# A load of two input tiles moved into the middle of five transposed weight loads, and a fourth matmul pair moved behind a tile's last one

## The chip, the cores and the metric

The kernel runs on one core of one Trainium2 chip. Its time is the device time of one execution in microseconds: 271.55 us, the median of three runs (271.33 to 272.35). The profile shows another view of one execution: which engine did what, counted from the span's first instruction.

The engines are TensorE (PE for its matmuls, PEld for its weight loads), VectorE (DVE), ScalarE (ACT), GpSimd (POOL) and SyncE (SP). SP computes nothing here; it issues nearly all DMAs, one after the other, and the core's 16 DMA engines carry them out. Every DMA of this kernel's SP queue is split into 16 pieces, one for each DMA engine, and has landed when the last piece has.

## The reference, cut to what matters

One transformer block over x (2048 rows of 640, bf16): linear attention with 32 heads of 20 columns, then a gated feed-forward network.

```python
qkv = layernorm(x) @ wqkv                  # q, k, v: 32 heads x 20 columns
pq, pk = q @ w_phi, k @ w_phi              # per head, 20 x 20
phi_q = concat(softmax(pq), softmax(-pq));  phi_k = concat(softmax(pk), softmax(-pk))
kv = phi_k.T @ v;  z = sum of phi_k over the rows
o = (phi_q @ kv) / (phi_q @ z + 1e-6)
h = x + o @ wo
h2 = h + (gelu(layernorm(h) @ w_gate) * (layernorm(h) @ w_up)) @ w_down
```

## The kernel before, in words

The 2048 rows are 16 tiles of 128 rows, kept in SBUF as four groups `x_sb[0..3]` of four tiles; tiles 6 and 7 are `x_sb[1][:, 2:4, :]`. The work has three stages: k and v of all tiles (about the first 58 us), then the queries, the attention and the feed-forward network, in which attention of later tiles is woven between the feed-forward matmuls.

The change lies in the opening of the first stage. Since `w_phi` follows W_k directly, the kernel multiplies the two once, on the chip: `fold` (L232) takes the transposed W_k (`WkT`, loaded by `load_T`, L200 to L205) and writes the product to `Wk2`. WkT comes in five blocks of 128 rows, each by one transposing DMA of SP (L203). `fold(WkT, Wk2, False, (d,))` needs block d alone: six matmuls into a PSUM tile `wa` (L248), whose loaded weights are the block, and then one copy into chunk d of `Wk2`, by ACT for chunks 0, 1, 3 and 4 (L257) and by DVE for chunk 2 (L259). k of a tile is a sum over the five chunks of `Wk2`: `k_part(t, c)` (L326) issues the two matmuls of chunk c (L296, two halves of 320 columns) of tile t, so it can begin while later chunks are not folded yet. `k_tile(t)` (L331) issues chunk 4, which ends k of the tile, and ACT takes the two exponentials of the result (L340).

TensorE and SP run in the order in which the program is written (`manual_schedule`, L81), and so do the others inside L82. TensorE's order around the change is: fold 0, 1, 2; v of tile 3 (ten matmuls); fold 3; chunks 0 to 2 of k of tile 0 and chunk 0 of tile 1 (eight matmuls); fold 4; chunks 1 and 2 of k of tile 1, chunk 3 of tile 0, chunk 3 of tile 1, chunk 4 of tile 0, chunk 4 of tile 1; then v of tile 4, k of tile 2 and so on in turn.

SP's order is: x tiles 0 to 2, W_v in three loads, x tile 3 among them, x tiles 4 and 5, the five blocks of WkT, x tiles 6 and 7 (L470), the transposed load of the normalized tile 4 (L167, called from `ln_ap`), x tiles 8 and 9 (L475), the normalized tile 5, x tiles 10 and 11 (L487), the normalized tile 6, and so on. The transposed loads of L167 each wait for the normalization of their tile (by DVE or ACT); the loads of x wait for nothing but SP. Tiles 6 and 7 are first read by the statistics of `ln_st(6)` and `ln_st(7)` on DVE (L488, L489; the instructions have L121).

Of the kernel before, what the change touches and what calls it, by code (L numbers as in the profile page):

```python
# [17 lines left out]
def kernel(  # L18
# [12 lines left out]
    nc = tc.nc  # L31
# [8 lines left out]
    NC = D // P  # L40
# [32 lines left out]
    x_v = A_x.rearrange("b (p t) d -> p (b t) d", t=NT)  # L73
# [11 lines left out]
    x_sb = [const.tile([P, 4, D], BF16, name=f"x_sb{b}") for b in range(NB)]  # L85
# [25 lines left out]
    def gtile(name):  # L111
        return psG.tile([P, 2, 512], F32, name=name, tag="G")
# [46 lines left out]
    def transpose_to(dst, src, on_pe, on_dve=False):  # L159

        if on_pe:
            tp = psG.tile([P, 16, P], BF16, name="tp", tag="G")
            for c in range(NC):
                nc.tensor.transpose(tp[:, c, :], src[:, c * P:(c + 1) * P], ident)  # L164
            (nc.vector.tensor_copy if on_dve else nc.scalar.copy)(dst, tp[:, 0:NC, :])  # L165
        else:
            nc.sync.dma_start_transpose(dst, src)  # L167
# [15 lines left out]
    WkT = fp.tile([P, NC, D], BF16, name="WkT")  # L183
# [16 lines left out]
    def load_T(WT, i, *ds):  # L200

        for d in ds:
            nc.sync.dma_start_transpose(WT[:, :, d * P:(d + 1) * P], A_wqkv[d * P:(d + 1) * P, i * D:(i + 1) * D])  # L203

    load_T(WkT, 1, *range(NC))  # L205
    wo_v = A_wo.rearrange("(c p) n -> p c n", p=P)
    wg_v = B_w_gate.rearrange("(c p) n -> p c n", p=P)
    wu_v = B_w_up.rearrange("(c p) n -> p c n", p=P)
# [23 lines left out]
    def fold(WT, W2, quarters, ds=range(NC)):  # L232


        n, w = 1, HD
        runs = []
        for c in range(NC):
            lo, hi = H0[c] * Dh, (H0[c] + NH[c]) * Dh
            for r in range(2 * n):
                a, b = max(lo, r * w), min(hi, (r + 1) * w)  # L240
                if a < b:
                    runs.append((r // n, r, c, a, b))
        runs.sort()
        for d in ds:
            wa = gtile("wa")
            wr = wa.rearrange("p u (q x) -> p (u q) x", q=n)
            for i, (u, r, c, a, b) in enumerate(runs):
                nc.tensor.matmul(wr[:, r, a - r * w:b - r * w], lhsT=WT[:, c, d * P:(d + 1) * P],  # L248
                                 rhs=BD[:, c].rearrange("p a b -> p (a b)")[:, a - H0[c] * Dh:b - H0[c] * Dh],
                                 start=(i == 0 or runs[i - 1][0] != u),  # L250
                                 stop=(i + 1 == len(runs) or runs[i + 1][0] != u), skip_group_check=True)
            dst, src = W2[:, d, :].rearrange("p (u f) -> p u f", u=2), wr[:, :, 0:w]
            if quarters:
                dst = W2[:, d, :].rearrange("p (c u m f) -> p u m c f", c=NC, u=2, m=2)
                src = src.rearrange("p u (m c f) -> p u m c f", m=2, c=NC)
            if d in (QA if quarters else KA):
                nc.scalar.copy(dst, src)  # L257
            else:
                nc.vector.tensor_copy(dst, src)  # L259
# [15 lines left out]
    def ln_st(*tiles, act=True, between=None, log=False):  # L275
        for t, v in zip(tiles, ln_stats(p1, [x_sb[t // 4][:, t % 4, :] for t in tiles], "1", act, between, log)):
            lnp[t] = v

    def ln_ap(t, on_act=False, on_pe=False):
        ln = (ln_act if on_act else ln_dve)(p1, "1", *lnp[t])  # L280
        if on_pe:
            lnp[t] = ln
        else:
            transpose_to(LN1T[t // 4][:, :, t % 4 * P:(t % 4 + 1) * P], ln, False)

    def ln_tp(t, on_dve=False):
        transpose_to(LN1T[t // 4][:, :, t % 4 * P:(t % 4 + 1) * P], lnp[t], True, on_dve)
# [5 lines left out]
    def proj(ps, t, W, us=(0, 1), cs=None):  # L293
        order = [(u, c) for u in us for c in range(NC)] if cs is None else [(u, c) for c in cs for u in us]
        for u, c in order:
            nc.tensor.matmul(ps[:, u, 0:HD], lhsT=lnT(t, c), rhs=W[:, c, u * HD:(u + 1) * HD],  # L296
                             start=(c == 0), stop=(c == NC - 1))
# [3 lines left out]
    def v_mm(t, us=(0, 1)):  # L301
        if 0 in us:
            pv[t] = gtile("pv")
        proj(pv[t], t, Wv, us)
# [10 lines left out]
    def v_ev(t):  # L315
        nc.scalar.activation(vS[t % NV][:, :, 1:VC].rearrange("p (u h) f -> p u h f", u=2),
                             pv[t][:, :, 0:HD].rearrange("p u (h f) -> p u h f", f=Dh), ACTF.Copy,
                             scale=lnp[t][2] if t in CT else 1.0)
# [7 lines left out]
    def k_part(t, *cs):  # L326
        if 0 in cs:
            pks[t] = gtile("pk")
        proj(pks[t], t, Wk2, cs=cs)

    def k_tile(t):  # L331
        if t in pks:
            pk = pks[t]
            k_part(t, NC - 1)
        else:
            pk = gtile("pk")
            proj(pk, t, Wk2)
        Ek[t] = ev.tile([P, 2, D], BF16, name="E", bufs=10)
        for s in range(2):
            nc.scalar.activation(Ek[t][:, s, :].rearrange("p (u f) -> p u f", u=2), pk[:, :, 0:HD],  # L340
                                 ACTF.Exp, scale=((lnp[t][2], nrstd[t]) if t in CT else (1.0, -1.0))[s])
# [26 lines left out]
    def kv_tile(t):  # L368

        E = Ek[t].rearrange("p s (h f) -> p s h f", f=Dh)  # L370
        for i in range(QH):
            for r in range(4):
                h = r * QH + i
                nc.tensor.matmul(kvp[QUAD[r], :, i * Dh:(i + 1) * Dh], lhsT=vF[t % NV][:, h * VC:h * VC + 32],  # L374
                                 rhs=E[:, :, h, :], start=(i == t == 0), stop=(t == NT - 1), skip_group_check=True)
# [11 lines left out]
    def q_mm(j, part=(0, 1), kcs=range(NC)):  # L387

        if 0 in part and 0 in kcs:
            pqs[j] = gtile("pq")  # L390
        for i, bc in enumerate(QG[j]):
            if i not in part:
                continue
            b, c = divmod(bc, NC)
            for kc in kcs:
                nc.tensor.matmul(pqs[j][:, i, :], lhsT=Wq2[:, kc, c * P:(c + 1) * P], rhs=LN1T[b][:, kc, :],  # L396
                                 start=(kc == 0), stop=(kc == NC - 1))

    def q_exp(j, signs=(0, 1)):
        for s in signs:  # L400
            nc.scalar.activation(Eq[j][:, :, s, :], pqs[j][:, 0:len(QG[j])], ACTF.Exp, scale=(1.0, -1.0)[s])  # L401
# [13 lines left out]
    def ln_a(t):  # L415

        ln = p1.tile([P, D], BF16, name="ln1", bufs=3)
        nc.vector.tensor_scalar(ln, x_sb[0][:, t, :], va[t][:, 0:1], va[t][:, 3:4], op0=ALU.add, op1=ALU.mult)
        return ln
# [47 lines left out]
                                op0=ALU.mult, op1=ALU.add)  # L467
    ln_st(4, act=False, between=lambda: ln_ap(3, on_pe=True))
    ln_tp(3, True)
    nc.sync.dma_start(x_sb[1][:, 2:4, :], x_v[:, 6:8, :])  # L470
    v_ev(2)
    fold(WkT, Wk2, False, (0,))
    fold(WkT, Wk2, False, (1,))
# [8 lines left out]
    fold(WkT, Wk2, False, (4,))  # L482
    k_part(1, 1, 2)
    k_part(0, 3)
    k_part(1, 3)
    ln_ap(5)
    nc.sync.dma_start(x_sb[2][:, 2:4, :], x_v[:, 10:12, :])  # L487
    ln_st(6)  # L488
# [5 lines left out]
    for t in range(NT):  # L494
        if t == T3:
            kvp = gtile("kvp")[:, 0, 0:2 * QF].rearrange("p (s f) -> p s f", s=2)
        late = t in (1, 2, 3, 4)
        if 0 < t < NT - 6 and not late:
            ln_ap(t + 6, on_act=True)
        k_tile(t)  # L500
        if t == 0:
            ln_ap(6)
            nc.sync.dma_start(x_sb[3][:, 0:2, :], x_v[:, 12:14, :])
        if t in FQ:
            fold(WqT, Wq2, True, [i for i, f in enumerate(FQ) if f == t])
        for i in KVG.get(t, ()):
            kv_tile(i)
        for j in range(len(QT)):
            if t == QT[j]:
                q_mm(j)  # L510
                q_exp(j)
                if j == 0:
                    nc.gpsimd.tensor_copy(Wg[:, 0, 0:1], Eq[j][:, 0, 1, 0:1])
                for i in KVQ.get(j, ()):
                    kv_tile(i)
        if 0 < t < NT - 3:
            v_mm(t + 3)
        if late:
            ln_ap(t + 6, on_act=True)
        if t == 1:  # L520
            nc.sync.dma_start(x_sb[3][:, 2:4, :], x_v[:, 14:16, :])
        if 0 < t < NT - 3:
            v_ev(t + 3)
        for i in ST.get(t, ()):
            ln_st(i, i + 1)
        k_norm(t)
        load_T(WqT, 0, *[i for i, f in enumerate(LQ) if f == t])
        if t == 10:
            transpose_to(LN1T[0][:, :, P:2 * P], ln_a(1), False)
        if t == 13:  # L530
            ln_ap(0, on_act=True)
        if t == 8:
            for z in KT:
                nc.gpsimd.memset(z, 0.0)
        if t == 5:
            nc.sync.dma_start(Wo, wo_v)
# [401 lines left out]
```

## Time and profile before

| | us |
|---|---|
| median of three runs (lowest, highest) | 271.55 (271.33, 272.35) |
| the profiled execution's own time | 272.35 |
| its span, first to last instruction | 270.6 |
| TensorE matmuls busy | 266.1 (98%) |
| VectorE, ScalarE, GpSimd busy | 173.9, 138.6, 101.2 |
| granted TensorE clock | 1.00 |

The table of loads below is from the trace's records of SP's issues and of the landings, one landing for each of the 16 pieces. "Most pieces" are the first to the fifteenth.

| load | SP issues it, us | most pieces landed by | last piece landed |
|---|---|---|---|
| x tiles 4, 5 | 4.15 | 9.87 | 9.88 |
| WkT block 0 | 4.63 | 10.55 | 10.56 |
| WkT block 1 | 6.57 | 11.25 | 11.26 |
| WkT block 2 | 7.88 | 12.08 | 12.11 |
| WkT block 3 | 9.72 | 13.15 | 13.17 |
| WkT block 4 | 11.04 | 14.03 | 15.54 |
| x tiles 6, 7 | 12.36 | 15.56 | 16.25 |
| normalized tile 4, transposed | 13.81 | 16.81 | 16.81 |
| x tiles 8, 9 | 15.07 | | 18.18 |
| normalized tile 5, transposed | 15.88 | | 19.72 |

How to read the profile's lines: a group gives a line of the program, an engine, an operation, what it writes and reads, and how often it ran. In a timeline the first two numbers are the start and how long the group took from its first to its last instruction; matmuls are pipelined, so such a row overlaps with the next. In the chain of work that ended last, each piece begins where the one before it left off, and that is the clock by which the prediction counts TensorE's work. DMA lines give the median time from SP's issue to the last piece.

### The profile page before, as it was taken

To read this page: it belongs to the slowest core of one execution; us is meant where nothing else is said; L and a number is where in the kernel's file an instruction comes from. 1 tells how busy PE (TensorE), PEld (TensorE's weight loads), DVE (VectorE), ACT (ScalarE), POOL (GpSimd) and SP (SyncE) were. 2 spreads that over 40 slices of the span, in tenths; PEclk is the share of its full clock that TensorE was granted. 3 is DMA by queue.
4 is the path that set the end of the run, shared out by engine and by line. 5 is a ranking of instruction groups with operands and counts; after the bars stand their busy time and mean duration, and the time that the engine had idled before them with its cause. 6 is when DMAs were issued, how large, how long until landed. Compare 5 with 4: busy or idle time off the path is not lost.

```text
span 270.6 us, 7029 instructions
## 1 busy us (share of the span) xinstructions
PE 266.1 (98%) x2857; PEld 172.0 (64%) x2857; DVE 173.9 (64%) x347; ACT 138.6 (51%) x249; POOL 101.2 (37%) x238
## 2 busy tenths in 40 slices
PE   8999999999999999999999999999999999999995
PEld 6777777765455887788755455775555476444574
DVE  5789999996877767876566783568673332333322
ACT  5779997877789675245541356421544300322100
POOL 5448898887002335376211564014661100000000
DMA  6987489213864442432301222203222101000011
GB/s 187 206 199 169 81 210 96 46 37 85 326 201 112 157 101 55 68 78 50 51 27 51 48 50 48 50 3 75 76 46 51 24 24 51 24 0 0 4 48 48
DMA packets 45264, 22.10 MB, mean 82 GB/s; under 512 B 37808, under 2 KB 43184, under 8 KB 45232
## 3 DMA queue, kind: packets, MB, share of 16 engines
q1 hardware_dynamic: 44576, 21.64, 33.5%
q8 instruction: 22, 0.36, 0.6%
q10 hardware_dynamic: 656, 0.03, 0.2%
q14 instruction: 10, 0.08, 0.1%
HBM read 10.18 MB, written 2.62 MB: 47 GB/s over the span
## 4 chain that ended last, share of the span: by engine, by line
PE 96%; DMA 2%; SPq 0%; DVE 0%; issue 0%
PE gu L768 39%; PE pd L790 19%; PE pq L396 8%; PE pk L296 8%; PE po L708 8%; PE pv L296 7%; DMA Wv<-in_A_wqkv_dram 2%; PE kvp L374 2%; PE pv L312 2%; PE ab L619 1%; PE wa L248 1%; PE ab L586 1%; PE tp L164 0%; SPq L193 0%; SPq L190 0%; SPq L189 0%
## 5 line engine op out<-in xcount | busy, mean ns | idle before, releaser
L771 ACT ACTIVATE g<-gu 128x512 bf16<-128x512 f32 (+1 forms) x60 | 30.4, 510 | 74.0 <-PE gu L768 73.2
L774 DVE TENSOR_TENSOR GT<-gu,g 128x512 bf16<-128x512 f32 (+1 forms) x60 | 34.3, 579 | 46.8 <-PE gu L768 38.6
L768 PE MATMUL gu<-LN2T,Wg 128*128 128x512 bf16 (+1 forms) x300 | 61.8, 337 | 0.0
L768 PE MATMUL gu<-LN2T,Wu 128*128 128x512 bf16 (+1 forms) x300 | 61.8, 336 | 0.0
L790 PE MATMUL pd<-Wd,GT 128*128 128x320 bf16 (+4 forms) x396 | 53.9, 295 | 0.0
L790 PEld LDWEIGHTS <-GT 128*128 128x128 bf16 x396 | 37.6, 98 | 14.5 <-DVE GT L774 0.2
L768 PEld LDWEIGHTS <-Wu 128*128 128x128 bf16 x300 | 29.4, 98 | 22.6
L768 PEld LDWEIGHTS <-Wg 128*128 128x128 bf16 x300 | 29.1, 98 | 21.2
L296 PEld LDWEIGHTS <-LN1T 128*128 128x128 bf16 x290 | 28.0, 98 | 10.4
L355 POOL TENSOR_TENSOR E<-E,rs 128x640 bf16<-128x640 bf16 x25 | 31.7, 1295 | 4.4 <-DVE rs L351 2.8
L792 DVE TENSOR_TENSOR y<-pd,x_sb 128x320 bf16<-128x320 f32 (+4 forms) x33 | 15.8, 480 | 24.1 <-PE pd L790 24.1
L708 PE MATMUL po<-Wo,oT 128*128 128x320 bf16 x160 | 24.5, 299 | 0.0
L296 PE MATMUL pk<-Wk,LN1T 128*128 128x320 bf16 x160 | 24.4, 299 | 0.0
L396 PE MATMUL pq<-LN1T,Wq 128*128 128x512 bf16 x100 | 22.9, 379 | 0.0
L347 DVE TENSOR_REDUCE sk<-E 128x64 f32<-128x1280 bf16 x16 | 22.9, 1430 | 0.0
L401 ACT ACTIVATE Eq<-pq 128x1024 bf16<-128x1024 f32 (+1 forms) x26 | 19.9, 831 | 2.8 <-PE pq L396 2.7
L340 ACT ACTIVATE E<-pk 128x640 bf16<-128x640 f32 x28 | 19.1, 769 | 3.0 <-PE pk L296 3.0
L708 PEld LDWEIGHTS <-oT 128*128 128x128 bf16 x160 | 15.6, 98 | 7.3 <-ACT oT L165 0.2
L296 PE MATMUL pv<-Wv,LN1T 128*128 128x320 bf16 x130 | 19.8, 299 | 0.0
L151 ACT ACTIVATE ln<-x_sb,v,rstd 128x640 bf16<-128x640 bf16 x14 | 12.9, 920 | 13.0 <-POOL v L747 12.9
L396 PEld LDWEIGHTS <-Wq 128*128 128x128 bf16 x100 | 9.4, 98 | 10.3
L683 DVE TENSOR_TENSOR tt<-AB,w 128x1280 bf16<-128x1280 f32 x10 | 15.1, 1505 | 0.4 <-POOL w L676 0.3
(120 smaller groups left out, 291.4 us busy)
## 6 DMA issues: line engine op xcount, KB each, us to landing
out_dram<-y SPq DMA_DIRECT2D x15, 160.0 KB, 1.8
x_sb<-in_A_x_dram SPq DMA_DIRECT2D x6, 320.0 KB, 3.3
Wd<-in_B_w_down_dram SPq DMA_DIRECT2D x1, 1440.0 KB, 6.8
Wg<-in_B_w_gate_dram SPq DMA_DIRECT2D x1, 1152.0 KB, 7.3
Wu<-in_B_w_up_dram SPq DMA_DIRECT2D x1, 1152.0 KB, 5.6
Wo<-in_A_wo_dram SPq DMA_DIRECT2D x1, 800.0 KB, 5.0
Wg<-in_B_w_gate_dram SPq DMA_DIRECT2D x1, 768.0 KB
Wu<-in_B_w_up_dram SPq DMA_DIRECT2D x1, 768.0 KB, 9.1
```

What stands on the lines that cost most here:

```text
L296: nc.tensor.matmul(ps[:, u, 0:HD], lhsT=lnT(t, c), rhs=W[:, c, u * HD:(u + 1) * HD], start=(c == 0), stop=(c == NC - 1))
L340: nc.scalar.activation(Ek[t][:, s, :].rearrange("p (u f) -> p u f", u=2), pk[:, :, 0:HD], ACTF.Exp, scale=((lnp[t][2], nrstd[t]) if t in C ...
L347: nc.vector.reduce_sum(sk, Ek[t].rearrange("p s (h f) -> p (s h) f", f=Dh), axis=AX.X)
L355: eng.tensor_tensor(e, e, rs[:, s * H:(s + 1) * H, None].to_broadcast([P, H, Dh]), ALU.mult)
L396: nc.tensor.matmul(pqs[j][:, i, :], lhsT=Wq2[:, kc, c * P:(c + 1) * P], rhs=LN1T[b][:, kc, :], start=(kc == 0), stop=(kc == NC - 1))
L401: nc.scalar.activation(Eq[j][:, :, s, :], pqs[j][:, 0:len(QG[j])], ACTF.Exp, scale=(1.0, -1.0)[s])
L708: nc.tensor.matmul(pos[u], lhsT=st[t][:, c, :], rhs=Wo[:, c, u * HD:(u + 1) * HD], start=(c == 0), stop=(c == NC - 1))
L768: nc.tensor.matmul(gu[i][:, 0:n], lhsT=W[:, c, f * P:(f + 1) * P], rhs=LN2T[b][:, c, a0:a1], start=(c == 0), stop=(c == NC - 1))
L771: nc.scalar.activation(g[:, 0:n], gu[0][:, 0:n], ACTF.Gelu_apprx_tanh)
L774: nc.vector.tensor_tensor(st[b, "g", f][:, a0:a1], gu[1][:, 0:n], g[:, 0:n], ALU.mult)
L790: nc.tensor.matmul(pd[:, 0:f1 - f0], lhsT=st[b, "g", f][:, tl * P:(tl + 1) * P], rhs=Wd[:, f, f0:f1], start=(f == 0), stop=(f == NF - 1), ...
L792: nc.vector.tensor_tensor(y[:, f0:f1], pd[:, 0:f1 - f0], x_sb[b][:, tl, f0:f1], ALU.add)
```

## The change

The load of x tiles 6 and 7 is issued by SP after the third block of WkT and before the fourth, where it used to follow the fifth block. On TensorE, the two matmuls of chunk 3 of k of tile 1 are issued behind chunk 4 of k of tile 0, where they used to stand ahead of it. No instruction is added or taken away.

```diff
-    load_T(WkT, 1, *range(NC))
+    load_T(WkT, 1, 0, 1, 2)
+    nc.sync.dma_start(x_sb[1][:, 2:4, :], x_v[:, 6:8, :])
+    load_T(WkT, 1, 3, 4)
...
     ln_tp(3, True)
-    nc.sync.dma_start(x_sb[1][:, 2:4, :], x_v[:, 6:8, :])
     v_ev(2)
...
     k_part(0, 3)
-    k_part(1, 3)
     ln_ap(5)
...
         k_tile(t)
         if t == 0:
+            k_part(1, 3)
             ln_ap(6)
```

## The prediction

> **What bounds the kernel now.** I read the page first: engine shares, then the chain of work that ended last.
>
> ```profile
> span 270.6 us, 7029 instructions
> ...
> PE 266.1 (98%) x2857; PEld 172.0 (64%) x2857; DVE 173.9 (64%) x347; ACT 138.6 (51%) x249; POOL 101.2 (37%) x238
> ...
> PE 96%; DMA 2%; SPq 0%; DVE 0%; issue 0%
> ```
>
> TensorE is busy for 98% and carries 96% of the chain. Next, the waits of TensorE alone, and its busy time in two stretches (columns: stretch, its length, busy time of PE, PEld, DVE, ACT and POOL with counts, granted clock, DMA share, GB/s).
>
> ```profile
> PE pv L312 <- DMA Wv<-in_A_wqkv_dram: 0.9, 1, 0.9
> PE wu L228 <- PEq L922: 0.8, 1, 0.8
> ...
> 7.40:20.00 12.60, 12.60 (x117) 9.61 (x117) 10.12 (x27) 8.93 (x16) 5.94 (x19) 1.00 0.95 198
> 20.00:60.00 40.00, 40.00 (x574) 29.09 (x572) 39.21 (x57) 36.00 (x56) 34.00 (x41) 1.00 0.59 109
> ```
>
> Its only waits lie before 7.41 us; from there it has no gap until the last output at 267.8. So nothing after 7.41 can be gained by bringing data earlier, and whatever TensorE is made to wait there is added in full to the end: no later gap takes it up. I therefore read every edit as "does TensorE wait for it?". The timeline around the change, for SP and for TensorE's weight loads:
>
> ```profile
> 4.63 7.69 SPq L203 DMA_TRANSPOSE WkT<-in_A_wqkv_dram  x5
> 12.36 0.58 SPq L470 DMA_DIRECT2D x_sb<-in_A_x_dram  x1
> 13.81 1.21 SPq L167 DMA_TRANSPOSE LN1T<-ln  x1
> ...
> 14.25 0.43 PEld L248 LDWEIGHTS <-WkT 128*128 128x128 bf16 x6
> ...
> 15.65 0.43 PEld L248 LDWEIGHTS <-WkT 128*128 128x128 bf16 x6
> ```
>
> The loads in flight at SP's 12.36, and the DMA queues from 13.2 to 14.6:
>
> ```profile
> x_sb<-in_A_x_dram SPq DMA_DIRECT2D x1, 320.0 KB, 3.9
> WkT<-in_A_wqkv_dram SPq DMA_TRANSPOSE x1, 4.5
> ...
> q8 instruction: 1, 0.02, 5.3%
> ```
>
> Block 4 lands 4.5 us after its issue, at 11.04 + 4.5 = 15.54, and its weights are loaded from 15.65: it is just in time already. The q8 line is one fetch of instructions: 5.3% of 16 engines times 1.4 us is 1.19 us on one DMA engine. The trace has it from 13.31 to 14.50. Fifteen pieces of block 4 had landed by 14.03, the sixteenth at 15.54, 1.51 later; of x 6/7 the last piece was 0.69 late (16.25 against 15.56).
>
> **How late the blocks may land.** In the chain, fold 3 begins at 14.54 and fold 4 at 15.95. One weight load takes 0.098, and from a semaphore to TensorE's reaction goes some 0.05 (the normalized tile 3 is ready at 11.25 + 0.45 = 11.70, its weight load starts at 11.75). So block 3 costs nothing until 14.54 - 0.15 = 14.39 and block 4 until 15.80. Before, block 3 (13.17) has 1.22 us of slack, block 4 has 0.26.
>
> **Edit 1, SP.** Issuing the x load takes SP 0.58, with the step to the next 0.62. It goes from 12.36 to about 9.72 (block 3's issue now); blocks 3 and 4 move to 10.34 and 11.66, and SP is free at 12.94. The next entry, the normalized tile 4, waits for DVE until 13.81 anyway (0.87 to spare), so it and all SP entries behind it stay. SP alone costs block 3 0.62 of its 1.22, block 4 0.62 of its 0.26.
>
> **Edit 1, the DMA engines.** Here the cost is not shown by one row, so I bound it. Lower end: the x load ahead costs only SP's slip; block 3 lands at 13.79, in time; block 4 keeps its regular gap behind block 3 (14.03 - 13.15, 0.88), 14.67, also in time: 0. For the other values I take the rows where plain and transposed loads follow each other. Plain behind transposed: x 6/7 landed 15.56 - 14.03 = 1.53 behind block 4, so here 12.11 + 1.53 = 13.64 (issue plus 3.9 gives 13.62, the same). Transposed behind plain, last piece to last piece: block 0 behind x 4/5 0.68, tile 4 behind x 6/7 0.56, tile 5 behind x 8/9 1.54. So block 3 lands at 14.20 to 15.18, with 0.68 at 14.32: alone that is at the edge of 14.39. Then the instruction fetch. It is in step with TensorE's own instruction count (22 fetches of 16 KB), and TensorE's order is unchanged until fold 3, so I expect it at 13.31 again; now block 3, not block 4, is on the way. A late piece was 0.69 and 1.51 late; the mean, 1.10, puts block 3 at 15.42. TensorE then waits 15.42 - 14.39 = 1.03 us at fold 3. The upper end is 13.64 + 1.54 + 1.51 = 16.69, a wait of 2.30. I take 1.03, since the nearest rows (same fetch, same engine, neighbouring loads) carry it.
>
> [...]
>
> Block 4 behind it: its regular gap of 0.88 gives at most 16.30, and fold 4, itself 1.03 later, needs it by 16.83: 0.53 to spare. If the fetch strikes block 4 instead, 14.32 + 0.88 + 1.10 = 16.30 against 15.80: 0.50 at fold 4 and nothing at fold 3. The cases are alternatives; I count one.
>
> What comes earlier gains nothing: x 6/7 land at 13.64 to 14.7, DVE's statistics want them at 15.85, so DVE's wait of 0.42 goes. But DVE's next result for TensorE, tile 6, is read at about 23.3 with TensorE never waiting. The normalized tile 4 (landed 16.81, needed for v of tile 4 at 17.89) has 0.93 to spare; it now follows transposed loads and TensorE needs it 1.03 later: 0.
>
> **Edit 2.** Chunk 3 of tile 1 was cover between fold 4 and the first use of chunk 4. Chunk 4 is ready 16.30 + 0.69 = 16.99, with the step 17.04; counted from fold 4's end (15.95 + 0.32 = 16.27) that is 0.77. Ahead of it stood eight matmuls of 0.136, 1.09; now six, 0.82. Cover remains, by 0.05 us, and ACT, idle 0.43 before that copy, is not held up by anything new: 0. If the cover failed, the whole price would be a few hundredths; with all of it gone, 0.77 - 0.82 + 0.27, some 0.2. k of tile 0 ends 0.27 earlier, so ACT's exponentials start earlier: no gain, as TensorE waits for none of them.
>
> **Sum.** 1.03 + 0 + 0 = 1.0. The profiled execution took 272.35 (span 270.6 and 1.75 around it) and would take 273.4; it is the slowest of the three runs, 0.80 above their median. On the median: 271.55 + 1.03 = 272.6 us, 0.4% slower. What a measurement of this kernel tells from no change is about 0.5%, 1.36 us.
>
> **The rivals.** *Hidden (not slower).* The switch costs less or the fetch misses block 3: it lands by 14.39. For it: 14.32 without the fetch, SP's slip alone leaves 0.60. Against: the fetch, and the margin of 0.07. Time: 271.55, within 0.3 either way. It decides as soon as block 3's last piece lands before 14.39.
>
> *Slower by more than 1.36.* Block 3's last piece after 15.75, by the long switch (1.54, tile 5 behind x 8/9) plus the late piece, up to 16.69: 271.55 + 2.30 = 273.85; the middle of 1.36 to 2.30 gives 273.4. For it: that row exists, and the fetch would now lie across both. Against: the other two switches took less than half, and tile 5's load was itself issued only 0.8 after the x load.
>
> *The clock falls in the wait.* TensorE's wait of 0.85 us before 7.41 left the granted clock at 1.00, so a wait of 1 should too; I give it a part of the slower case only.
>
> *Faster by more than 1.36.* It would need a wait on TensorE that the profile of before lacks. DVE is busy 39.21 of 40 us between 20 and 60 and would start 0.42 earlier, but TensorE waits for it nowhere.
>
> **How the numbers follow.** Forecast, a wait of 0.3 to 1.36 at fold 3 or 4: 0.47. Hidden: 0.22. Slower by more than 1.36: 0.28. Faster by more: 0.03. Faster 0.03, same 0.47 + 0.22 = 0.69, slower 0.28. The likeliest case's time is 272.6. Its own range is 271.85 to 272.9. The range for 8 in 10 goes from 271.4 (hidden, less the 0.2 by which runs of before differ downward) to 273.6 (most of the slower case; its end of 273.85 is left out).
>
> **What would show it.** Right: SP's x load at 9.7; TensorE with a wait on WkT of about 1 us before fold 3, the only new one; DVE's wait of 0.42 on x gone; block 3's last piece near 15.4 with fifteen others near 14.3; the stretch after 20 us unchanged and shifted. Wrong: no wait on WkT in TensorE's list (hidden), waits at both folds, a clock below 1.00, or a wait on chunk 4 of `Wk2` above 0.1 (edit 2's cover).

## The result, and the profile after

The changed kernel takes 273.08 us (median of six runs, 272.49 to 273.20) against 271.56 for before (271.33 to 272.35): a ratio of 1.005, 95% interval 1.0034 to 1.0065. Measured a second time beside before it was 273.06 against 271.70, the same ratio (1.0036 to 1.0065). The change makes the kernel 1.4 to 1.5 us slower, some 0.5%.

The page of the changed kernel, the same lines as were shown of before:

```profile
span 271.2 us, 7029 instructions
...
PE 265.8 (98%) x2857; PEld 171.4 (63%) x2857; DVE 173.8 (64%) x347; ACT 138.7 (51%) x249; POOL 101.2 (37%) x238
...
PE 93%; SPq 3%; DMA 2%; issue 0%; DVE 0%
```

TensorE does no less and no more. But the chain that ended last, which in the profile of before left SP's queue at W_v, now follows that queue up to the fourth block of W_k (block 3, counted from 0). Three of TensorE's four waits in the changed kernel:

```profile
PE wa L250 <- DMA WkT<-in_A_wqkv_dram: 1.1, 1, 1.1
PE wu L230 <- PEq L923: 0.8, 1, 0.8
PE pv L314 <- DMA Wv<-in_A_wqkv_dram: 0.5, 1, 0.5
```

The first line is new: one wait of 1.1 us, for a block of W_k, at a fold. (The fourth wait, 0.2 us, lies at the start, on the normalization of the first tiles; the second profile of the changed kernel does not have it.)

The spans of the two first profiles differ by only 0.6 us, where the medians differ by 1.5. The profile of before that the prediction read was of an execution with a late start: the last piece of the first W_v load landed at 7.36, in all later profiles at 6.7 or before. So a second profile of each kernel was taken (below); its two executions took 271.89 and 273.15 us, 1.26 apart, and they are what the terms are measured on. The chain of before, second profile (start, length, what):

```profile
10.41 4.81 DMA WkT<-in_A_wqkv_dram
15.27 0.49 PE wa L248 x6
15.75 1.63 PE pk L296 x12
17.38 1.36 PE pv L296 x10
```

and of the changed kernel, second profile:

```profile
9.54 5.56 DMA WkT<-in_A_wqkv_dram
15.15 0.49 PE wa L250 x6
15.64 1.09 PE pk L298 x8
16.73 0.32 PE wa L250 x6
17.04 1.75 PE pk L298 x12
18.80 0.27 PE pv L298 x2
```

The first `wa` row of before is fold 4, that of the changed kernel is fold 3, each behind the block that it waits for: at the same time as before was folding its last block, the changed kernel folds its fourth. v of tile 4 begins at 18.80 in place of 17.38.

### The profile page after: what moved, and what is told of

Read it like the earlier page. It is cut to its first block, busy times and chain, and to the rows that moved or that the text cites. A ratio compares the mean times of both kernels' runs of the same rounds, so it can differ in the third digit from the quotient of the medians.

```text
span 271.2 us, 7029 instructions
## 1 busy us (share of the span) xinstructions
PE 265.8 (98%) x2857; PEld 171.4 (63%) x2857; DVE 173.8 (64%) x347; ACT 138.7 (51%) x249; POOL 101.2 (37%) x238
## 4 chain that ended last, share of the span: by engine, by line
PE 93%; SPq 3%; DMA 2%; issue 0%; DVE 0%
PE gu L769 38%; PE pd L791 19%; PE pq L398 8%; PE pk L298 8%; PE po L709 8%; PE pv L298 6%; DMA WkT<-in_A_wqkv_dram 2%; PE kvp L376 2%; SPq L203 2%; PE ab L620 1%; PE ab L587 1%; PE wa L250 1%; PE tp L164 0%; SPq L206 0%; SPq L195 0%
## 5 line engine op out<-in xcount | busy, mean ns | idle before, releaser
L684 DVE TENSOR_TENSOR tt<-AB,w 128x1280 bf16<-128x1280 f32 x10 | 15.1, 1506 | 0.4 <-POOL w L677 0.3
```

## The experiments

In all of them nothing of the computation is changed or left out. Each is given with its time, that of before in the same minutes, and the ratio with its 95% interval.

**1. The load alone**, the matmul pair in its old place:

```diff
-    load_T(WkT, 1, *range(NC))
+    load_T(WkT, 1, 0, 1, 2)
+    nc.sync.dma_start(x_sb[1][:, 2:4, :], x_v[:, 6:8, :])
+    load_T(WkT, 1, 3, 4)
```

> The load of x 6/7 ahead of W_k's fourth block alone; the matmul pair stays in its old place. Theory (the load order carries the loss: TensorE waits for block 3 at fold 3): a wait on WkT of about 1.1 us at fold 3, no new wait on chunk 4; 1.2 to 1.4 us above before, 272.8 to 273.0, ratio 1.0045 to 1.005. Rival (the moved pair carries it): no change, 271.6.

Measured 272.76 against 271.77, 1.0042 (1.0028 to 1.0055), with a wait of 1.3 us on WkT at fold 3. The loss of 0.99 is less than the 1.2 to 1.4 expected.

**2. The pair alone**, loads in the old order:

```diff
-    k_part(1, 3)
     ln_ap(5)
...
         if t == 0:
+            k_part(1, 3)
             ln_ap(6)
```

> The matmul pair moved alone; the loads stay in the old order. Theory: no wait on WkT; the weight load of chunk 4 of tile 0 waits some 0.15 us for ACT's copy of chunk 4, 0.1 us above before, 271.7, ratio 1.000 to 1.001. Rival (the moved pair carries the loss): 1.2 to 1.5 us above before, 273.0.

Measured 271.78 against 271.77, 1.0007 (0.9997 to 1.0017). Most of the loss comes with the load. The pair has a price too small for the time to show, but the chain shows it. The twelve matmuls behind fold 4, with the pair in its old place (experiment 1):

```profile
16.77 1.63 PE pk L298 x12
```

and moved (experiment 2):

```profile
15.70 1.75 PE pk L296 x12
```

So 0.12 us; the row has 1.75 or 1.76 in both profiles of the changed kernel too, and 1.63 in both of before.

**What the block waits for.** The block that fold 3 waited for landed at 14.89 and 15.11 in the two profiles of the changed kernel; by the prediction's regular rows it would have been in by 14.3. It landed 1.08 and 1.04 us after the end of an instruction fetch, one transfer of 16 KB, counted in the q8 line. In the first profiles of both kernels this fetch begins with 105 matmuls and 106 weight loads of TensorE behind it, at 13.31 in before and at 12.65 in the changed kernel, so it kept its place among TensorE's instructions, not its time. For block 3 in the second profile of the changed kernel, its time from issue to landing, and the DMA queues from 12.5 to 14.2:

```profile
WkT<-in_A_wqkv_dram SPq DMA_TRANSPOSE x1, 5.6
...
q8 instruction: 1, 0.02, 5.3%
```

The fetch began at 12.62 and took 1.45 us, to 14.07: 5.3% of 16 engines times 1.7 us is 1.44 us on one DMA engine, its whole length. Three pieces of block 3 had landed by 13.06, the other thirteen came between 14.82 and 15.11. Two causes could hold the block: theory A, the fetch; theory B, the switch between plain and transposed loads. To tell them apart, the next runs move the fetch by changing the number of the warm-up matmuls at the very start and not their columns: in before's first profile one of 512 columns took 0.427 us to the next and one of 128 columns 0.107; from these, equal time for equal columns is an estimate.

**3. The fetch later:**

```diff
-    warm(*[512] * 2, *[P] * 28)
+    warm(*[512] * 2, *[2 * P] * 14)
```

> The changed kernel, with the 28 warm-up matmuls of 128 columns at the start as 14 of 256 columns: the same TensorE time, 28 instructions fewer, so that the instruction fetch that now falls at 12.65 comes some 28 instructions later in TensorE's order, 1 us or more. Theory A (the fetch holds block 3): block 3 lands by 13.6 to 13.8, TensorE waits under 0.2 us at fold 3, and the time falls to about 272.0. Theory B (the switch from plain to transposed loads holds it): block 3 still lands near 14.8, the wait stays at 1.1 us and the time at 273.1.

The fetch came at 13.69. Block 3 landed at 13.76, 4.2 us after its issue, and the wait is gone: the chain passes fold 3 with 0.04 between it and the matmuls before, though with no slack, as its own six matmuls still take 0.49.

```profile
12.41 1.36 PE pv L298 x10
13.77 0.04 issue
13.80 0.49 PE wa L250 x6
```

Same loads, same order, same switch: A holds, B does not. Block 4 landed at 14.52, 0.83 after the start of this fetch and before its end, so this fetch did not hold a block that was that close to landing. In no profile here did a piece of a block land later than that and less than 0.7 behind the fetch's end. The time, though, was 272.85 against 271.77 (1.0049, 1.0031 to 1.0067), not 272.0. V of tile 4 began at 17.45, 1.35 earlier than in the changed kernel; the later fetches moved as well, and one at 98.16 caught a transposed load of o, which took 4.4 us in place of its usual 2.4, landing 1.1 behind that fetch's end, and made TensorE wait 0.6. (The expectation of experiment 5 puts this wait near 77 us by mistake; it ends at 100.4.)

**4. The fetch earlier**, `warm(*[P] * 36)`:

> The changed kernel, with the two warm-up matmuls of 512 columns as eight of 128: the same TensorE time, 12 instructions more, so that the fetch comes about 0.6 us earlier, near 12.0. Theory A (the fetch holds block 3, for a time that goes by the fetch's end): block 3 lands near 14.2, the wait at fold 3 falls to about 0.5 us, 272.5. Theory B (the switch): the wait stays at 1.1 us, 273.1.

The fetch did not come earlier (12.71; TensorE's own start was late in this profile, by waits of 0.7 and 0.5). Wait 1.2, time 273.11, 1.0052 (1.0038 to 1.0065): nothing told apart. That a fetch ahead of block 3 would free it was not shown.

**5. Before with the later fetch**, the control for 3:

> The kernel before, with the same warm-up as in the run with the late fetch (14 matmuls of 256 columns for 28 of 128). Theory A: the fetch comes near 13.7, after block 4's packets, no wait at either fold; the later fetches move too, and the wait on the transposed o of 0.6 us near 77 us that the late-fetch run showed appears here as well. So the time is that of the late-fetch run less the 0.12 us of the moved pair, 272.5 to 272.8. If the later loss there came from the moved x load instead: 271.5.

Measured 272.60 against 271.72, 1.0030 (1.0019 to 1.0042), inside what A expected: the warm-up edit alone costs 0.9 us. The wait on o that A expected was 0.3 and not 0.6. No wait on W_k; instead the fetch, now at 14.33, fell on SP's next entries. SP's issue of x tiles 8 and 9 took 1.39 in place of 0.58, the normalized tile 5 behind it came late, and TensorE waited elsewhere:

```profile
PE po L708 <- DMA oT<-o: 0.3, 1, 0.3
PE pv L296 <- DMA LN1T<-ln: 0.3, 1, 0.3
```

Matmul by matmul, this execution was 0.30 ahead of before's second profile at fold 4, 0.11 behind it at v of tile 5 and 0.28 behind from 54 us on, and 0.75 behind from the matmuls of o at 100 us on. That is what the two executions differ by (272.64 and 271.89).

With the fetch moved in both kernels, v of tile 4 begins at 17.45 with the change (experiment 3) and 0.38 earlier without it, where the second profiles differ by 1.42. So about 1 us of the loss is where the fetch falls. The times, 272.85 and 272.60, differ by 0.25; their intervals are too wide to tell that from nothing, and the waits further on differ too.

**6. The load one block later**, between blocks 3 and 4:

```diff
-    load_T(WkT, 1, 0, 1, 2)
+    load_T(WkT, 1, 0, 1, 2, 3)
     nc.sync.dma_start(x_sb[1][:, 2:4, :], x_v[:, 6:8, :])
-    load_T(WkT, 1, 3, 4)
+    load_T(WkT, 1, 4)
```

> The changed kernel with the load of x 6/7 one block later, between the fourth and fifth block of W_k. Theory A: block 3 has landed by 12.9 and is clear of the fetch (near 12.6), no wait at fold 3; block 4 is on the way at the fetch and lands 2.2 to 2.5 us behind its start, 14.9 to 15.1, against a need at about 15.05: a wait of 0 to 0.3 at fold 4, the time 271.8 to 272.1. Theory B (each switch from plain to transposed delays the block behind it by more than 1 us): a wait of 1 us or more at fold 4, 272.9.

Block 3 landed at 12.20, clear of the fetch (12.88 to 13.88). The load under way at the fetch was now the plain one, of x tiles 6 and 7: fifteen of its pieces landed from 14.68 to 14.84, up to 0.96 behind the fetch's end, and block 4 followed at 15.44.

```profile
10.86 4.58 DMA WkT<-in_A_wqkv_dram
15.48 0.49 PE wa L250 x6
```

So the fetch held a plain load here, as it held a transposed one. TensorE waited 0.3 at fold 4, inside the 0 to 0.3 of A and far from the 1 us of B, though block 4 itself came later than A's 14.9 to 15.1. The time of 272.61 (271.72; 1.0035, 1.0024 to 1.0045) is above the 271.8 to 272.1 expected. Its eight runs lie in two groups, near 272.3 and near 272.9; the profile is of one at 272.33, so what the upper group adds stays open.

**7. Four kilobytes in place of 320**, an extra small load between blocks 2 and 3, the x load in its old place:

```diff
+    tiny = const.tile([P, 16], BF16, name="tiny")
+    load_T(WkT, 1, 0, 1, 2)
+    nc.sync.dma_start(tiny, x_v[:, 6, 0:16])
+    load_T(WkT, 1, 3, 4)
```

> The kernel before, with an extra load of 16 columns of one tile (4 KB, into a tile that nothing reads) between the third and fourth block: SP's issue and the switch without the bytes. Theory A: block 3 is 0.5 to 0.6 later than before; whether TensorE waits depends on whether its packets are through by the fetch near 12.6: then no wait at fold 3 and under 0.5 at fold 4, 271.8 to 272.2. Theory B (the switch): a wait near 1.1 at fold 3 as in the changed kernel, 272.8.

No wait at fold 3. Block 3's time from issue, and SP's issue of x tiles 6 and 7 behind the blocks:

```profile
WkT<-in_A_wqkv_dram SPq DMA_TRANSPOSE x1, 2.9
...
12.13 1.80 SPq L473 DMA_DIRECT2D x_sb<-in_A_x_dram  x1
```

Block 3 landed at 12.47, no later than in before's second profile (12.79). With the switch but without the bytes block 3 needs 2.9 us from its issue, with 320 KB ahead 4.2 (experiment 3). Both landed in the first 0.31 us of the fetch and were not held by it. Behind another block, with no switch, it needed 3.3 to 4.0 (experiments 6 and 2). So the bytes cost 1.3 us in these two profiles, the switch nothing that can be seen. The time, 272.47 (271.72; 1.0026, 1.0016 to 1.0036), is above the 271.8 to 272.2 expected, and was lost later: the fetch, from 12.16, fell on SP's issue of x tiles 6 and 7, which took 1.80 in place of 0.58, and TensorE waited twice 0.3 for normalized tiles.

**8. The fetch half as far**, `warm(*[512] * 2, *[P] * 16, *[2 * P] * 6)`:

> The changed kernel with 16 warm-up matmuls of 128 columns and 6 of 256 in place of 28 of 128: 12 instructions fewer, so that the fetch comes some 0.5 us later, near 13.1, while block 3 is still on the way. Theory A: block 3's last piece lands 2.2 to 2.5 us behind the fetch's start, at 15.3 to 15.6, so the wait at fold 3 grows to 1.5 to 1.9 us, although the fetch is later. Theory B: the wait stays at 1.1 us.

The fetch began at 13.30 and ended at 14.32; thirteen pieces of block 3 were in by 13.59, the last at 15.14. Wait 1.3, time 273.23 (271.72; 1.0055, 1.0041 to 1.0069). The block is late by the fetch though most of it had come, but the wait did not grow to 1.5: this run alone would not settle A.

**9. Half the bytes**, x tile 6 ahead of block 3, tile 7 in the old place:

> The changed kernel with half the load ahead of block 4 (index 3): x tile 6 alone (160 KB); tile 7 goes back to the old place. If the bytes ahead of the block set the wait, it falls by some 0.4 us, half of what 320 KB take on the engines, and the time to about 272.6. If the fetch sets it: block 3 is still on the way at the fetch (12.4 to 12.7), lands 2.2 to 2.5 us behind the fetch's start, near 14.9, and the wait stays at 1.1 to 1.3 us, 272.9 to 273.1. If half the bytes bring block 3 in ahead of the fetch, as 4 KB did, no wait at fold 3 and 272.2.

Fourteen pieces of block 3 landed by 12.55, the last two at 14.25 and 14.27, 2.16 behind the start of a fetch that came early (12.11). The weight load of fold 3:

```profile
14.31 0.31 PEld L250 LDWEIGHTS <-WkT 128*128 128x128 bf16 x6 [1.12 <-DMA WkT<-in_A_wqkv_dram]
```

TensorE waited 0.8. (Its list of waits puts this down to ACT's copy of v of tile 3, which ended in the same moment. Fold 3 does not need that copy: in before's first profile fold 3 began at 14.54 and the copy at 14.58.) The time was 272.37 against 271.96, 1.0015 (1.0003 to 1.0027). The wait is below the 1.1 to 1.3 expected of the fetch, and by wait and time alone the run fits the other expectation, that the bytes set the wait. (The 0.4 expected is half of what 320 KB took on the engines: 128 packets of 2560 bytes, 102 ns each at the median of before's first profile, are 0.82 us on 16 engines.) For the fetch speaks that the held pieces came 1.7 us behind the other fourteen and 0.8 behind the fetch's end.

**10. The two kernels again:**

> The kernel before, unchanged, for a second profile. If the profile of before that the prediction read was an execution with a late start (W_v's last piece at 7.36 against 6.3 to 6.7 in all the others), this one has TensorE at v of tile 4 near 17.3 in place of 17.9, a span near 269.9, and a wait of 0.1 to 0.3 us on block 4 at fold 4. If the late start is the rule for this order of loads: 17.9 and no wait.

> The changed kernel, unchanged, beside before on the same chip and in the same minutes. Sum of the terms as measured so far: a wait at fold 3 of 1.1 to 1.3, 0.17 more for fold 3's own six matmuls, 0.12 for the moved pair, less the 0.2 that before waits at fold 4: 1.2 to 1.4 us above before, ratio 1.0045 to 1.005.

Before: 271.57 (271.70 for before in the same minutes; 0.9996, 0.9987 to 1.0005), span 270.2, v of tile 4 at 17.38, the weight load of fold 4 waiting 0.45. The late start was that one execution's. Changed: 273.06, as expected.

**11. A try at less waiting:** W_v's first load ahead of x tile 2, in before.

> The kernel before, with the first load of W_v ahead of x tile 2. TensorE's wait on W_v at 6.6 to 7.4 shortens by up to SP's 0.43 us; the later waits (block 4 behind the fetch) may take some of it back. Gain carried through: 271.3 to 271.5, ratio 0.998 to 0.999. If fold 4 waits for block 4 instead: 271.7, no change.

Measured 272.43 against 271.70, 1.0024 (1.0013 to 1.0034). The gain expected did not come: the wait on W_v went, but the normalization of tile 2 came late and TensorE waited 0.7 for it. No kernel tried here beats before.

## Why the prediction was right, and where its terms were off

The measured 273.08 is inside 271.4 to 273.6, on the side forecast. The forecast time was 272.6, a loss of 1.03; measured 1.36 and 1.52 in the two comparisons. That is past the likeliest case's own range (271.85 to 272.9), on the edge between "within 0.5%" (0.69) and "slower" (0.28).

The **cause was named rightly**: TensorE waits once, at fold 3, for the last pieces of block 3, which the instruction fetch holds back. The mechanism stood in the sum as the fetch that now strikes block 3 in place of block 4. Its **size was off**: I added a mean lateness of pieces (1.10) to a regular landing (14.32). The records say otherwise. In the first and second profiles of both kernels and in experiments 1, 2 and 4 the block under way at the fetch landed its last piece 1.04 to 1.08 us after the fetch's end, whatever its regular landing:

| profile | fetch, us | block | last piece | behind the fetch's end |
|---|---|---|---|---|
| before, first | 13.31 to 14.50 | 4 | 15.54 | 1.04 |
| before, second | 12.97 to 14.14 | 4 | 15.22 | 1.08 |
| changed, first | 12.65 to 13.81 | 3 | 14.89 | 1.08 |
| changed, second | 12.62 to 14.07 | 3 | 15.11 | 1.04 |
| load alone | 12.37 to 13.75 | 3 | 14.84 | 1.08 |

(Experiments 8 and 9 had 0.82 and 0.80 for block 3, experiment 6 had 0.96 for x tiles 6 and 7; block 4, which came behind in experiments 6 and 7, 1.56 and 1.48.) By that row the prediction's own fetch would have given 14.50 + 1.05 = 15.55 and a wait of 1.16; a fetch of 1.45 in place of 1.19 covers the rest of the 1.35 measured.

The margin without the fetch, 14.32 against 14.39, came out near (experiment 3: block 3 at 13.76, fold 3 at 13.80), partly by luck. Block 3 landed 2.77 behind block 2 and not 2.21; but block 2 came 1.12 earlier than in the profile that the prediction read, and fold 3 only 0.74 earlier.

What the folds waited for was the last piece: fold 4 of before's second profile waited for the one at 15.22 with fifteen in by 13.69.

**"Transposed behind plain", the switch,** was read wrongly. The 0.56 to 1.54 that I took for its price are no price of a switch: in before's first profile blocks 1 to 3 landed 0.70 to 1.06 behind the block ahead, with no switch between, and with a switch but 4 KB ahead block 3 came sooner after its issue, not later (2.9 us against 3.3 to 4.0, experiment 7). The time of the lower end, no change, still did not come: 320 KB ahead in the queue, with which block 3 landed at 13.76 where no fetch held it (experiment 3), were enough to carry it into the fetch at 12.62 (second profile). No run here measures the two kinds of load against each other.

**Block 4, "0.26 us of slack",** held in the late start alone. In before's second profile fold 4 already waits: its matmuls took 0.49 in place of 0.32 and began some 0.12 late; the first weight load, at 15.26, started 0.01 ahead of its matmul, where in the first profile it started 0.13 ahead (15.65 and 15.78). The changed kernel does not pay this 0.29 at fold 4, but pays the 0.17 at fold 3.

**Edit 2, "cover remains, by 0.05",** failed: it cost 0.12. I counted the cover up to the first matmul of chunk 4. The wait stands on the weight load ahead of it, which in before's first profile starts 0.13 ahead of it (17.05 and 17.18). ACT's copy and the weight loads in the changed kernel's second profile:

```profile
17.08 0.69 ACT L259 CAST Wk<-wa 128x640 bf16<-128x640 f32 x1 [0.71 <-PE wa L250]
...
17.83 0.23 PEld L298 LDWEIGHTS <-LN1T 128*128 128x128 bf16 x2 [0.17 <-issue]
```

The copy ends at 17.77, the weight load starts at 17.83 after 0.17 idle, and the matmul behind it comes 0.12 late. The profile calls the idle time "issue" and names no releaser, so no list of waits puts it down to the copy. That it is the copy follows from the times: here, in the first profile and in experiment 2, the weight load starts 0.05 to 0.06 behind the copy's end.

**"No later gap takes it up"** was nearly right. The matmuls of `kvp` near 53 us took 1.58 in before's second profile and 1.47 in the changed kernel's:

```profile
52.68 1.58 PE kvp L374 x160
```

```profile
54.06 1.47 PE kvp L376 x160
```

Those near 40 us went from 1.33 to 1.30. TensorE had been held there by some 0.14 that the waits did not list, and gave that much back.

The sum on the second profiles: 1.35 (fold 3) + 0.17 (its weight loads) + 0.12 (pair) - 0.29 (fold 4 of before) = 1.35. TensorE reached fold 0 at 11.26 and 11.30, 0.04 apart, and v of tile 4 began 1.42 later. Less 0.14 given back, 1.28; the executions differ by 1.26.

As predicted, DVE's wait of 0.42 on x tiles 6 and 7 went and gained nothing (a wait of 0.95 on tiles 8 and 9 took its place), and the clock stayed at 1.00.

## What to carry to other kernels

A load's slack is counted to its last piece, and against whatever else uses the DMA engines at that moment: here a load with about a microsecond to spare was pushed by 320 KB into an instruction fetch, and TensorE waited 1.35 us for it. Before moving a load ahead of one that the busiest engine needs, look for the fetches in the DMA queues and ask which load will be on the way then; and take the slack from more than one execution, since one late start hid a wait of 0.45 us on a weight load here. Cover for a wait is counted to the weight load, which here started 0.13 us ahead, not to its matmul: counted to the matmul the prediction had 0.05 to spare, and the move cost 0.12.

## What the runs showed of the hardware that was not expected

A fetch of 16 KB on one DMA engine (5.6% of 16 engines times 1.3 us, 1.17 us) held nearly all pieces of a transposed load: in the changed kernel's first profile fifteen of block 3's pieces landed between 14.67 and 14.89, one at 13.36, with the fetch from 12.65 to 13.81. In before only one piece of block 4 was held, to 15.22 against 13.69 (second profile). In both, the pieces that were not held landed within 0.72 of the fetch's start, so how many were held went, in these two, with how far the load had come. In experiment 6 the fetch held a plain load: fifteen of its pieces landed from 14.68 to 14.84, behind a fetch from 12.88 to 13.88. Why one fetch on one DMA engine held fifteen pieces was not settled.

The number of instructions at the start of TensorE's program, 14 matmuls of 256 columns in place of 28 of 128, changed before by 0.9 us (experiment 5). With it the fetches moved against the loads: the first from 12.97 to 14.33, and one from 95.38 to 98.12, onto a transposed load of o that TensorE then waited 0.3 us for.
